# A gated mix of sliding-window attention and a SwiGLU block: x's casts ahead of V's copies, x's sums split on VectorE alone, the gate moved into the last group, more buffers for the projections, a third hidden tile prepared early

## The chip, the cores and the metric

The kernel runs on one core of one Trainium2 chip. The metric is the device time of one execution in microseconds (us).

## What is computed

```python
x = A_x                                             # 1 x 2048 x 512, fp32
g = sigmoid((x * gate_w).sum(-1, keepdims=True))
q, k, v = split_heads(x @ wqkv)                     # 32 heads of 16
s = where(0 <= i - j < 256, q @ k.T / 4, -1e9)      # sliding window of 256
a = (softmax(s) @ v) @ wo
b = (silu(x @ w_gate) * (x @ w_up)) @ w_down        # 512 -> 1792 -> 512
out = g * a + (1 - g) * b
```

## The kernel before

Every fp32 operand of a projection is cut into two halves of precision: `split(hi, lo, src, hi_eng, lo_eng)` (L65) writes a rounded copy hi (a cast) and the rest lo = src - hi (a subtraction), and a product is made of three matmuls: hi hi, hi lo and lo hi. The program is one stream per engine, written out by hand. Each engine runs its own stream in order and waits by semaphores, so an instruction that waits holds up everything behind it on its engine. The same is true of SP, whose queue issues nearly all DMAs, and of POOL, whose queue issues the writes of V and of the attention output. A tile from a pool with n buffers waits until the tile that had its buffer n allocations ago has been read for the last time; when a pool is closed, what is allocated in its place waits for its last readers, DMAs among them. PSUM has four pairs of 128x512 banks: pa, pb, ps1, ps2.

The work comes in five stages.

1. **V** (L169 to L274). x arrives transposed in four chunks c of 512 positions, each in four tiles k. `split_x(c, k)` splits one: the cast on ScalarE (ACT), the subtraction on VectorE (DVE). V's product of block b of 128 positions is twelve matmuls (`vproj`); blocks 0 to 3 need chunk 0, blocks 8 to 11 chunk 2, and so on. `put_v(b)` copies a block from PSUM into one of two buffers `vs` on ACT, and after each second block POOL writes the buffer to DRAM (`vd`). `v_extra(b)` slips other work between: the splits of chunks 2 and 3, the sums of x (`diffs`, on DVE, four tiles for each half a of the positions), their splits (`put_t(a, n, ...)`), and the splits of the first weights (`op_a`, `op_s`, `op_z`).
2. **Q and K** (L364 to L462). Pairs p of head groups, four in all; each pair is a Strassen-Winograd scheme of seven products (numbers 1 to 7) for each half a, six matmuls each. Results are copied out of PSUM by ACT (`copied`, tiles `u`), summed on DVE (`add_to`), split into a `cx` tile (`put_c`: cast on ACT, subtraction on POOL, or on DVE for the product that is taken from PSUM) and written to DRAM (`xd`, 512 KB each) by SP. A product that accumulates into a bank again waits for the copy. The next pair's weights are fetched into the one tile `rw`. The gate's sums (`gate_fetch`, `gate_block`: a 256 KB load of x's rows `xn` and one DVE operation) run here too, four blocks in each pair, and `gate_end` closes them. In the last pair the q and k operands of group 0 begin to be stacked: POOL fills the tiles with constants (`constant_rows`), SP reads `xd` into every fourth row (`stack`, six DMAs for each half and pair of heads).
3. **Start of the attention** (L657 to L676). 64 ticks. In each, three steps of the SwiGLU projections (`stream`, `unit`; results go to DRAM as `raws` through five `ev` buffers), and from tick `WAIT` on, the scores of group 0, whose only use is the row maximum (`stage1`, L557; the maximum on DVE with a mask, L559).
4. **Attention** (L723 to L752). Eight groups of four heads, 16 query blocks t in each, four ticks hd for each block: scores of the next group for their maximum (`stage1`), transposed scores of this one and their exponent (`stage2`, L596, L598), masks on POOL, steps of the projections, and after four blocks the products with V (`av`, L620), taken out of PSUM by `evacuate` and normalized by `finish`. The last group has no scores for a maximum; in it the first eight tiles of `w_down` are split and the first two hidden tiles are made (`tile_early`).
5. **Down projection** (L865 to L898): 56 hidden tiles, each twelve matmuls, and the attention's output projection among them.

A unit of the projections is made by `lanes`: the 128 rows of a matmul are cut into two halves of 64 that run side by side on two result tiles, with one turn over each. The second turn must stand behind a point that the first one's results are known to have passed, and that point is an instruction of the attention's stream:

```python
if second and i == 0:
    tc.add_manual_dep(mm.ins, BEHIND[mark[0]].ins.name, SYNC, reason="the first turn is over")
```

Of the kernel before, what the change touches and what calls it, by code (L numbers as in the profile page):

```python
# [33 lines left out]
def gated_mix(ctx, tc, xT, xn, wqk, wv, wo, wgu, wd, gw, out):  # L34
# [179 lines left out]
    for k in range(NK):  # L214
        split_x(1, k)
    for b in range(4):
        put_v(b, first[b])

# [25 lines left out]
    def v_extra(b):  # L244
        if 4 <= b < 6:
            for k in range(2):
                split_x(2, 2 * (b - 4) + k)
            if b == 4:
                TD.extend(diffs(0))
        elif b < 8:  # L250
            put_t(0, (1, 0)[b - 6], TD[(1, 0)[b - 6]], nc.gpsimd)
        elif b < 10:
            for k in range(2):
                split_x(3, 2 * (b - 8) + k)
        elif b < 12:
            put_t(0, b - 8, TD[b - 8], nc.vector)
        elif b == 12:
# [4 lines left out]
        elif b < 15:  # L262
            put_t(1, (1, 0)[b - 13], TD[(1, 0)[b - 13]], nc.gpsimd)
        else:
            for n in (2, 3):
                put_t(1, n, TD[n], nc.vector)
# [39 lines left out]

    gp = ExitStack()
    gpool = gp.enter_context(tc.tile_pool(name="gpool", bufs=1, side="right"))  # L310
    gwb = gpool.tile([P, D], F32, name="gwb")
    nc.sync.dma_start(gwb, gw[None, :].to_broadcast([P, D]))
    XN = {}

    def gate_fetch(b):
        XN[b] = gpool.tile([P, D], F32, name="xn", bufs=2)
        nc.sync.dma_start(XN[b], xn[b * P:(b + 1) * P])

    def gate_block(b):
        junk = gpool.tile([P, D], F32, name="junk")  # L320
        nc.vector.scalar_tensor_tensor(junk, XN.pop(b), 1.0, gwb, op0=ALU.mult, op1=ALU.mult,
                                       accum_out=gate[:, b:b + 1])

    def gate_end():
        nc.scalar.activation(gate, gate, AF.Exp, scale=-1.0)
        nc.vector.tensor_scalar(gate, gate, 1.0, None, op0=ALU.add)
        nc.vector.reciprocal(gate, gate)
        nc.vector.tensor_scalar(igate, gate, -1.0, 1.0, op0=ALU.mult, op1=ALU.add)
# [21 lines left out]
    def put_c(p, r, c, src, psum):  # L350
        g, (hf, cc) = 2 * p + r, divmod(c, 2)

        def halve():
            cx = cx_tile()
# [70 lines left out]
    for p in range(NP):  # L425
# [34 lines left out]
    gate_end()  # L460
    gp.close()
# [10 lines left out]
    with ExitStack() as A:  # L472
# [3 lines left out]

        constant_rows(1, 0, ("q00", "k00", "q01", "k01"), nc.gpsimd)
        stack(0, 1)
        for hf in range(2):
            constant_rows(hf, 1, ("q10", "k10", "q11", "k11"), nc.gpsimd)  # L480
# [43 lines left out]

        def unit(key):

            def done(hf):
# [5 lines left out]
                return copies  # L533
            (a0, a1), (b0, b1) = (lanes(name, [products(key, 2 * hf + m) for m in range(2)], done(hf))
# [124 lines left out]
        TICKS, WAIT = 16 * NSLOT, 7  # L659
        for n in range(TICKS):  # L660
# [5 lines left out]
            if n == WAIT:  # L666
                stack(1, 0)
            if n == 30:
                stack(1, 1)
# [7 lines left out]

        def wd_early(k, f, piece):
            at(k, lambda: later(4, load_wd(f, pieces[piece], kept())))
# [3 lines left out]
        RAW_AT, TILE_AT = (14, 8), (12, 10)  # L683
        TILE = [None, None]
# [18 lines left out]

        g7 = (G - 1) * NB
        early = chain(tile_early(0), tile_early(1))
# [9 lines left out]
        for n in range(12):  # L715
            at(4 * (g7 + 11) + 1 + 2 * n, lambda: run(early, 1))
# [216 lines left out]
```

## Time and profile before

| | us |
|---|---|
| median of three runs | 859.45 (858.97 to 868.62) |
| the profiled execution | 856.95 |
| its span, first to last instruction | 855.0 |
| PE busy in the span | 824.7 (96%) |
| DVE, ACT, POOL busy | 589.3, 465.2, 385.6 |

The timeline gives start, duration, engine, line and operation, names and shape, and in brackets the idle time before an instruction with what ended it; "x6" is six instructions merged into a row. The chain of waits gives start, duration and what ran or was waited for. Windows give the busy time of each engine in a stretch, the granted clock of TensorE, the busy share of the DMA engines and their GB/s.

### The profile page before, as it was taken

The page shows a single profiled execution, that of the slowest core. Times are in us where ns is not written, and L with a number is a line of the kernel's source. Part 1 is how long each engine was busy: PE and PEld are TensorE (multiplying, and loading weights), DVE is VectorE, ACT ScalarE, POOL GpSimd, SP SyncE. Part 2 cuts the span into 40 slices and gives each one's busy share as a digit, 9 for nine tenths or more (in the row PEclk, how much of TensorE's full clock was granted, in tenths as well). Part 3 has the DMA queues.
Part 4 walks back from the last instruction along what each step waited for, and adds up shares of the span by engine and source line. Part 5 has one row for each costly group of instructions (what it writes and reads, how often), then busy time and mean ns, then how long its engine had stood idle before and what let it go on. Part 6 is the DMA issues. An engine that isn't in the chain of part 4 may idle for free.

```text
span 855.0 us, 21084 instructions
## 1 busy us (share of the span) xinstructions
PE 824.7 (96%) x7945; PEld 681.3 (80%) x7945; DVE 589.3 (69%) x1503; ACT 465.2 (54%) x947; POOL 385.6 (45%) x671
## 2 busy tenths in 40 slices
PE   9796999699999999999999999999998999999998
PEld 7685888588888878787888888888876788888886
DVE  3665664487788888888888888888377764363533
ACT  5452453114676767666666666666766453443441
POOL 5333455603566657656566566565763121101020
PEclk9898999799999999999999999999999999999999
DMA  8335888674255535535455265442547985284741
GB/s 301 99 98 171 308 303 304 230 243 159 71 174 169 166 123 191 179 127 171 161 171 180 90 198 178 143 143 95 178 156 265 299 261 197 81 299 115 232 136 49
DMA packets 78821, 154.21 MB, mean 180 GB/s; under 512 B 12352, under 2 KB 16832, under 8 KB 78720
## 3 DMA queue, kind: packets, MB, share of 16 engines
q1 hardware_dynamic: 74752, 138.97, 49.8%
q0 software_dynamic: 3968, 13.90, 4.5%
q8 instruction: 62, 1.02, 0.5%
q14 instruction: 39, 0.32, 0.1%
HBM read 88.34 MB, written 64.49 MB: 179 GB/s over the span
## 4 chain that ended last, share of the span: by engine, by line
PE 87%; DMA 5%; issue 3%; DVE 3%; SPq 1%; ACT 1%; POOL 1%; DVEq 0%; ACTq 0%; POOLq 0%
PE pa L514 18%; PE pb L514 18%; PE ps L620 9%; PE ps L557 7%; PE ps L81 5%; PE ps L80 5%; PE ps L79 5%; PE ps L596 5%; PE ps L389 3%; PE pb L389 2%; PE pa L389 2%; PE pb L80 2%; PE pb L81 2%; PE pb L79 2%; DMA vd<-vs 1%
## 5 line engine op out<-in xcount | busy, mean ns | idle before, releaser
L559 DVE CUSTOM_DVE_ANT_0 ps<-ps,mask 128x384 f32<-128x384 f32 (+2 forms) x512 | 271.6, 543 | 45.2 <-PE ps L557 34.3
L598 ACT ACTIVATE pt<-ps 128x384 f32<-128x384 f32 (+2 forms) x512 | 238.1, 478 | 80.8 <-PE ps L557 31.9
L596 PE MATMUL ps<-q,k 64*128 64x384 f32 (+2 forms) x512 | 172.0, 347 | 0.8 <-ACT pt L598 0.7
L557 PE MATMUL ps<-k,q 63*128 63x384 f32 (+2 forms) x512 | 163.5, 339 | 0.1
L600 POOL TENSOR_SCALAR_AFFINE_SELECT pt<-pt 128x256 f32<-128x256 f32 x256 | 107.3, 419 | 108.4 <-ACT pt L598 103.3
L557 PEld LDWEIGHTS ps<-k,q 63*128 63x128 f32 x512 | 88.6, 185 | 30.4 <-DVE oe L634 10.8
L514 PE MATMUL pa<-xhi,wh 64*128 64x512 f32 x448 | 101.1, 399 | 8.6 <-DVE mx L559 8.6
L514 PE MATMUL pb<-xhi,wh 64*128 64x512 f32 x448 | 101.5, 394 | 0.0
L596 PEld LDWEIGHTS ps<-q,k 64*128 64x128 f32 x512 | 93.0, 184 | 9.9 <-ACT pt L598 5.8
L514 PE MATMUL pa<-xlo,wh 64*128 64x512 f32 x448 | 100.3, 397 | 0.0
L514 PE MATMUL pb<-xlo,wh 64*128 64x512 f32 x448 | 100.2, 393 | 0.0
L514 PE MATMUL pb<-xhi,wl 64*128 64x512 f32 x448 | 99.3, 391 | 0.0
L514 PE MATMUL pa<-xhi,wl 64*128 64x512 f32 x448 | 98.8, 395 | 0.0
L603 POOL TENSOR_SCALAR_AFFINE_SELECT pt<-pt 128x256 f32<-128x256 f32 x224 | 94.8, 423 | 0.0
L820 DVE TENSOR_TENSOR sg<-got,sg 128x512 f32<-128x512 f32 x53 | 47.1, 889 | 60.9 <-ACT sg L819 59.3
L620 PE MATMUL ps<-pt,vg 64*32 64x320 f32 (+4 forms) x2816 | 76.9, 348 | 0.0
L620 PEld LDWEIGHTS ps<-pt,vg 64*32 64x32 f32 x2816 | 50.7, 106 | 29.3 <-issue 8.4
L637 POOL TENSOR_TENSOR ob<-oe,ob 128x512 f32<-128x512 f32 x32 | 42.1, 1317 | 68.0 <-DVE oe L634 66.7
L559 DVE DVE_READ_ACCUMULATOR2_ANT mx<- 128x1 f32 x512 | 72.3, 141 | 0.0
L514 PEld LDWEIGHTS pa<-xhi,wh 64*128 64x128 f32 x448 | 52.4, 188 | 12.1 <-DVE mx L559 8.8
L67 ACT CAST hh<-sg 128x512 fp32r<-128x512 f32 x54 | 33.3, 617 | 42.9 <-PE ps L80 27.0
L514 PEld LDWEIGHTS pb<-xhi,wl 64*128 64x128 f32 x448 | 53.0, 185 | 3.6
(219 smaller groups left out, 1692.0 us busy)
## 6 DMA issues: line engine op xcount, KB each, us to landing
raws<-ev SPq DMA_DIRECT2D x112, 256.0 KB
got<-raws SPq DMA_DIRECT2D x106, 256.0 KB
xd<-cx SPq DMA_DIRECT2D x32, 512.0 KB
q<-xd SPq DMA_DIRECT2D x96, 128.0 KB
k<-xd SPq DMA_DIRECT2D x96, 128.0 KB
od<-oe POOLq DMA_DIRECT2D x32, 256.0 KB, 3.3
raw<-wgu SPq DMA_DIRECT2D x28, 256.0 KB
vd<-vs POOLq DMA_DIRECT2D x8, 672.0 KB, 4.5
```

The lines of the kernel that those rows point to most:

```text
L79: nc.tensor.matmul(ps, lh, rh, start=start and i == 0, stop=False, skip_group_check=skip)
L80: nc.tensor.matmul(ps, lh, rl, start=False, stop=False, skip_group_check=skip)
L81: nc.tensor.matmul(ps, ll, rh, start=False, stop=stop and i == n - 1, skip_group_check=skip)
L389: nc.tensor.matmul(ps, l[:, w], r[:, k], start=n in (1, 2, 5) and k == m == 0, stop=k == 1 and m == 2, skip_group_check=True)
L514: mm = nc.tensor.matmul(ps[me], w[r], x[r], start=not second and i == 0, stop=bool(second) and i == n - 1)
L557: nc.tensor.matmul(ps[:, :n], QT[g % 2][pr][r, q0:q0 + P], KT[g % 2][pr][r, k0:k0 + n], start=True, stop=True)
L559: mx = nc.vector.tensor_tensor_reduce(out=ps[:, :n], in0=ps[:, :n], in1=mask[:, 3 * P - n:], scale=1.0, scalar=NEG, op0=ALU.add, op1=ALU.m ...
L596: nc.tensor.matmul(ps[:, :n], KT[g % 2][pr][r, k0:k0 + P], QT[g % 2][pr][r, k0:k0 + n], start=True, stop=True)
L598: BEHIND.append(nc.scalar.activation(pt[:, j, :n], ps[:, :n], AF.Exp, scale=SCALE))
L600: nc.gpsimd.affine_select(out=pt[:, :, :P], in_=pt[:, :, :P], pattern=[[0, 2], [1, P]], compare_op=ALU.is_ge, fill=0.0, base=0, channel_mu ...
L603: nc.gpsimd.affine_select(out=pt[:, :, 2 * P:], in_=pt[:, :, 2 * P:], pattern=[[0, 2], [-1, P]], compare_op=ALU.is_ge, fill=0.0, base=-1, ...
L620: nc.tensor.matmul(AV[g, c][h][32 * j:32 * j + 32, q0 - c * CH:q1 - c * CH], VG[4 * g + kb // 4][o, kb % 4, 17 * j:17 * j + 32], PT[g, kb, ...
```

## The change

- In stage 1, `split_x` of chunks 1 and 2 stands ahead of the first four `put_v`, and that of chunk 3 right behind them. `v_extra` keeps the sums and their splits, and all of these have both subtractions and sums on VectorE; one split of a half stands at each of b = 6 to 9 and 12 to 15.
- The gate leaves stage 2. Its loads and sums are made around the last group, every fourth tick (sometimes third), with one buffer for x's rows; the operation comes three ticks behind its load.
- The tiles of `put_c` alternate between the four `cx` and four new `cy` buffers in a pool `more`.
- The first unit of the projections is made by `whole`, without turns: 48 steps of one full matmul. `WAIT` is 10 ticks for 7. Constant rows and stacks of groups 0 and 1 move from ahead of the loop into its ticks 1, 8, 10, 12 and 14.
- In the attention, where `av` stands, four steps of the projections move behind `evacuate`, and the tick behind them has none.
- One hidden tile is made in the last group by `tile_early`; two more by `tile_silu` when the last exponent is through. The down projection starts with three tiles ready for two.

```diff
-    for k in range(NK):
-        split_x(1, k)
+    for c in (1, 2):
+        for k in range(NK):
+            split_x(c, k)
     for b in range(4):
         put_v(b, first[b])
+    for k in range(NK):
+        split_x(3, k)
...
     def v_extra(b):
-        if 4 <= b < 6:
-            for k in range(2):
-                split_x(2, 2 * (b - 4) + k)
-            if b == 4:
-                TD.extend(diffs(0))
-        elif b < 8:
-            put_t(0, (1, 0)[b - 6], TD[(1, 0)[b - 6]], nc.gpsimd)
...
+        if b == 4:
+            TD.extend(diffs(0))
+        elif 6 <= b < 10:
+            n = (1, 0, 2, 3)[b - 6]
+            put_t(0, n, TD[n], nc.vector)
...
+        elif 11 < b:
+            n = (1, 0, 2, 3)[b - 12]
+            put_t(1, n, TD[n], nc.vector)
...
+    more = mp.enter_context(tc.tile_pool(name="more", bufs=1, side="right"))
+    def c_tile():
+        CX[0] += 1
+        return cx_tile() if CX[0] % 2 else more.tile([P, 2, CH], F32R, name="cy", bufs=4)
...
-            if i < 8 and i % 2 == 0:
-                gate_fetch(4 * p + i // 2)
-            if i in (4, 6, 8, 10):
-                gate_block(4 * p + i // 2 - 2)
...
-    gate_end()
-    gp.close()
+    mp.close()
     pro.close()
...
+        def whole(name, todos, done):
+            ps = [pp.tile([P, CH], F32, name=name) for _ in todos]
+            for t, todo in zip(ps, todos):
+                for i, (w, x) in enumerate(todo):
+                    nc.tensor.matmul(t, w, x, start=i == 0, stop=i == len(todo) - 1)
...
-        TICKS, WAIT = 16 * NSLOT, 7
+        TICKS, WAIT = 16 * NSLOT, 10
...
-            if n == WAIT:
-                stack(1, 0)
-            if n == 30:
-                stack(1, 1)
+            if n == 1:
+                constant_rows(1, 0, ("q00", "k00", "q01", "k01"), nc.gpsimd)
+                stack(0, 1)
+            if n in (8, 10, 12, 14):
+                hf, pr = divmod(n // 2 - 4, 2)
+                constant_rows(hf, 1, (f"q1{pr}", f"k1{pr}"), nc.gpsimd)
+                stack(1, hf, (pr,))
...
+        def gate_block(b):
+            t = osb.tile([P, D], F32, name="xn")
+            nc.sync.dma_start(t, xn[b * P:(b + 1) * P])
+            later(3, lambda: nc.vector.scalar_tensor_tensor(t, t, 1.0, gwb, op0=ALU.mult, op1=ALU.mult,
+                                                            accum_out=gate[:, b:b + 1]))
...
+        def tile_silu(n):
+            (gt, up), sg = GOT[n], kept()
+            TILE[n] = halves_of(pieces[TILE_AT[n]])
+            nc.scalar.activation(sg, gt, AF.Silu)
+            nc.vector.tensor_tensor(out=sg, in0=up, in1=sg, op=ALU.mult)
+            split(*TILE[n], sg, nc.scalar, nc.vector)
...
+        at(4 * g7 - 6, lambda: nc.sync.dma_start(gwb, gw[None, :].to_broadcast([P, D])))
+        for b in range(NB):
+            at(4 * g7 - 5 + 4 * b - b // 4, lambda b=b: gate_block(b))
+        at(4 * (g7 + NB - 1), gate_end)
...
-                n = (k + 1) * 9 // 4 - k * 9 // 4
-                if t < G * NB:
+                n = (2, 1, 4, 2)[hd] if values else (k + 1) * 9 // 4 - k * 9 // 4
+                if t < G * NB and not (values and hd == 2):
                     run(steps, n)
                 tick_end()
-                if hd == 1 and part == 0 and t:
+                if hd == 1 and values:
                     av(*divmod(d - 1, NCH))
                     run(FIN, 1)
                     evacuate(*divmod(d - 1, NCH))
+                    if t < G * NB:
+                        run(steps, 4)
...
-        fresh, waiting, ready = [], [(0, n, *TILE[n]) for n in range(2)], []
-        for c, n in seq[2:]:
+        fresh, waiting = [], [(0, n, *TILE[n]) for n in range(3)]
+        ready = [load_wd(8, pieces[8], raw2())]
+        for c, n in seq[3:]:
```

More of the change, by code (lines that the diff above doesn't have):

```diff
@@ L305, in prepare @@
         prefetch()
[L309 to L328, printed above, removed]
+    mp = ExitStack()
+    more = mp.enter_context(tc.tile_pool(name="more", bufs=1, side="right"))
+    CX = [0]
+    def c_tile():
+        CX[0] += 1
+        return cx_tile() if CX[0] % 2 else more.tile([P, 2, CH], F32R, name="cy", bufs=4)
     def fill_rows(t, value, hf, eng):
@@ L533, in done @@
                 return copies
+            if key == UNITS[0]:
+                return chain(*(whole(name, [products(key, 2 * hf + m) for m in range(2)], done(hf))
+                               for hf, name in enumerate(("pa", "pb"))))
             (a0, a1), (b0, b1) = (lanes(name, [products(key, 2 * hf + m) for m in range(2)], done(hf))
@@ L728, in gated_mix @@
             s2 = stage2(g, i) if t < G * NB else iter(())
+            values = part == 0 and t > 0
             for hd in range(4):
@@ L892, in gated_mix @@
                 attn_step(c, n - 8)
-            if len(waiting) > 1:
+            while len(waiting) > (1 if c or n > 5 else 2):
                 step(*waiting.pop(0))
```

47 lines of the change are left out of this document (22 added, 25 removed).

## The prediction

> **What bounds the kernel now.** I read the page first, then windows by stage, then the timeline of PE around each hole, then the other engines and the chain of waits there. Span, clock and GB/s are of the page; then four windows (columns: length, busy PE, PEld, DVE, ACT, POOL, clock, DMA share, GB/s).
>
> ```profile
> span 855.0 us, 21084 instructions
> ...
> PEclk9898999799999999999999999999999999999999
> ...
> GB/s 301 99 98 171 308 303 304 230 243 159 71 174 169 166 123 191 179 127 171 161 171 180 90 198 178 143 143 95 178 156 265 299 261 197 81 299 115 232 136 49
> ...
> 84.00:143.00 59.00, 59.00 (x262) 48.84 (x261) 36.12 (x67) 30.64 (x54) 32.76 (x25) 1.00 0.85 305
> ...
> 203.00:594.00 391.00, 390.81 (x5300) 325.48 (x5298) 329.17 (x1065) 264.13 (x581) 236.09 (x501) 1.00 0.47 152
> 594.00:651.00 57.00, 55.29 (x799) 44.70 (x796) 34.87 (x50) 38.23 (x89) 36.72 (x71) 1.00 0.47 161
> 651.00:678.00 27.00, 24.45 (x102) 18.53 (x103) 22.02 (x36) 13.45 (x23) 5.56 (x5) 1.00 0.93 311
> ```
>
> PE has no idle time in 84 to 143 and next to none in 203 to 594. So TensorE is the bound, its work hardly changes, and what there is to win lies in the holes: three before 164, and small ones behind 594 (57.0 - 55.29 = 1.7 us, 27.0 - 24.45 = 2.55 us). The clock digits dip in the second, fourth and eighth slice, behind the three holes. (A slice is 21.4 us.)
>
> **Term 1, the first hole (x's casts ahead, sums on VectorE).** PE's timeline, with one row of the chain for the pace:
>
> ```profile
> 11.25 1.36 PE pb L208 x6
> ...
> 30.35 0.39 PE L208 MATMUL pa<-wvl,xhi 128*128 128x512 f32 x1
> 33.83 0.79 PE L208 MATMUL pa<-wvh,xlo 128*128 128x512 f32 x1 [3.09 <-DVE xlo L70]
> ...
> 37.08 0.80 PE L208 MATMUL pa<-wvh,xlo 128*128 128x512 f32 x1 [1.60 <-DVE xlo L70]
> ...
> 41.65 0.39 PE L208 MATMUL pb<-wvh,xhi 128*128 128x512 f32 x1
> ```
>
> A 512-column matmul costs 1.36 / 6 = 0.227 us. Between the end of the one at 30.35 (30.58) and 41.65 stand 16 matmuls, block 8 from its third and block 9: 3.63 us of work in 11.07. The hole costs 7.44 us, of which 3.09 + 1.60 are waits for xlo and the rest, 2.7, is half speed behind them. Why xlo was late, on ACT, DVE and POOL:
>
> ```profile
> 23.93 0.59 ACT L183 COPY vs<-ps 128x512 f32<-128x512 f32 x1 [5.26 <-DMA vd<-vs]
> 24.41 1.14 ACT L67 CAST xhi<-k 128x512 fp32r<-128x512 f32 x2
> ...
> 26.28 1.22 DVE L193 TENSOR_TENSOR cx<-q,q 128x1024 f32<-128x1024 f32 x1
> ...
> 30.95 6.08 DVE L70 TENSOR_TENSOR xlo<-k,xhi 128x512 fp32r<-128x512 f32 x2
> ...
> 29.93 3.30 POOL L70 TENSOR_TENSOR q<-cx,q 128x1024 fp32r<-128x1024 f32 x1 [2.70 <-ACT q L67]
> ```
>
> The casts of chunk 2 stood behind block 4's copy, which waited 5.26 us for a write of V; on DVE the four sums came between; and the last two subtractions took 6.08 us for two, where a sum of double the size took 1.22, because they ran against POOL's. After the change the casts follow those of chunk 1, bound only by x's arrival: chunk 2 ends the first 16 transfers of 0.26 MB, 14 us at the 301 GB/s of the first slice, so with the start some 15.5; casts and subtractions end near 17, eleven us ahead of block 8, whose first matmul stands eight ahead of 30.35, at 28.5. The copies of blocks 0 to 3 slip 1 to 2 us; their banks are wanted by block 8 only. DVE takes four subtractions of some 1.22 us from POOL; its list up to the last block is then 16 of half that size, 16 of 1.22 and about 4 us for the weights, 34 us in 45. Block 15's half is due for product 7, seven us after V's end. So I cost all of this at nothing; the cover is those seven us of products; with it gone, it would be one subtraction, 1.2 us. **-7.4**, bounds -7.4 and -4.
>
> **Term 2, the second hole (the gate leaves SP).** PE, POOL, a step of the chain, SP and ACT:
>
> ```profile
> 63.18 0.39 PE L389 MATMUL ps<-xhi,al 128*128 128x512 f32 x1
> ...
> 77.72 1.22 PE L389 MATMUL pb<-k,sh 128*128 128x512 f32 x2 [6.66 <-ACT u L373]
> ...
> 83.56 0.62 PE L389 MATMUL pa<-k,zh 128*128 128x512 f32 x2
> ...
> 59.65 6.71 POOL L70 TENSOR_TENSOR q<-cx,q 128x1024 fp32r<-128x1024 f32 x2 [3.25 <-ACT q L67]
> ...
> 66.31 4.17 DMA vd<-vs
> ...
> 70.62 0.33 SPq L312 DMA_DIRECT2D gwb<-gw  x1
> 71.11 0.80 SPq L127 DMA_DIRECT2D rw<-wqk  x2
> ...
> 76.04 0.62 ACT L67 CAST ah<-rw 128x512 fp32r<-128x512 f32 x1 [6.80 <-DMA rw<-wqk]
> ```
>
> From 63.41 to 83.56 stand eight products of six matmuls, 10.88 us in 20.15: the hole costs 9.27. PE waited for a copy on ACT that stood behind a cast of the next weights, these had been fetched at 71.11 only, behind the gate's own load on SP, and that load took the place of V's buffers, whose last write left POOL at 66.31, after two subtractions of 6.71 us. The change takes away every link: no load for the gate here, no subtraction of these on POOL. What is late next is the first `cy` tile, which takes V's place now: from 41.65 on V has 72 matmuls, 16.3 us, so it ends at 58.0 - 7.4 = 50.5; its last write is issued by 52 and needs 4 to 5 us (4.17 above), and the `cy` cast belongs to the fourth product, four times 1.36 later, and stands behind a copy of the fifth: near 58. **-9.3**, bounds -9.3 and -6.
>
> **Term 3, the third hole (start of the attention).** PE, a step of the chain, DVE and ACT:
>
> ```profile
> 143.50 0.59 PE L514 MATMUL pa<-xhi,wh 64*128 64x512 f32 x2
> ...
> 149.09 0.29 PE L557 MATMUL ps<-k,q 63*128 63x128 f32 x2
> 157.94 0.79 PE L514 MATMUL pa<-xhi,wh 64*128 64x512 f32 x2 [8.56 <-DVE mx L559]
> ...
> 163.59 1.38 PE pb L514 x12
> ...
> 153.01 3.00 DVE L326 TENSOR_SCALAR gate<-gate 128x16 f32<-128x16 f32 x1 [7.68 <-ACT gate L325]
> ...
> 157.53 0.30 DVE L559 CUSTOM_DVE_ANT_0 ps<-ps,mask 128x128 f32<-128x128 f32 x1 [0.61 <-DMA xd<-cx]
> ...
> 152.24 0.62 ACT L67 CAST cx<-u 128x512 fp32r<-128x512 f32 x1 [3.93 <-DMA xd<-cx]
> ```
>
> A step takes 1.38 / 6 = 0.23. From the end of the scores at 149.2 to 163.59 stand twelve steps and two pairs of scores, 2.96 us in 14.39: 11.4 lost. A second turn waited for the first maximum; that one stood behind the gate's end on DVE, behind casts that waited for `cx` buffers, and last for the final `xd` write, since its own tile lies where stage 2's tiles lay. The change takes away the turns of unit 0 (33 steps, 7.6 us, come ahead of the first scores), the casts' waits (eight buffers) and the gate's end. **-11.4**, and two things are late next (SP's timeline, and the page's issues):
>
> ```profile
> 166.65 1.72 SPq L341 DMA_DIRECT2D q<-xd  x3
> ...
> xd<-cx SPq DMA_DIRECT2D x32, 512.0 KB
> ```
>
> First, the last writes. In new time stage 2 ends at 143.5 - 16.7 = 126.8. The last sum, cast and subtraction take 0.7 + 0.6 + 1.3, so the last five writes of 0.52 MB leave SP near 128 to 131, behind six stacks, and at 305 GB/s (84 to 143) need 8.6 us: landed at 137 to 139. The first maximum waits for that; PE needs it for the fifth score matmul, tick 15, behind 45 steps at 137.5, and the copies to `ev` need the same place by the 48th, 138.5. I take **+1.5**, bounds 0 and +4 (with half speed). Second, SP: 36 transfers of the stacks at 1.72 / 3 = 0.57 us each stand ahead of or between unit 0's four results now, 21 us from 130.5 on; the last result leaves near 152 and takes some 3.3 us (`od`, below), and unit 2, 108 steps and 25 ticks of scores in, needs that `ev` buffer's bank by 154.5. **+0.5**, bounds 0 and +3.
>
> The clock behind such waits: 3.09 us (of 30.35) was followed by half speed, 1.03 us (650.82, below) by none. At 1.5 us, nearer to the second, I take none; 2.7 more, as behind the first hole, is in the upper end. [...]
>
> **Term 4, attention.** Group by group PE does the same work. Moving four steps behind `evacuate` covers the wait of the following scores for the evacuation, but puts two score pairs next to each other, which then want two maxima in a row. Rows for this and the next two terms, from the page's groups, the waits (total, times, longest), the issues (the last number is from issue to landing), a window's groups (84 to 143) and the timeline:
>
> ```profile
> L559 DVE CUSTOM_DVE_ANT_0 ps<-ps,mask 128x384 f32<-128x384 f32 (+2 forms) x512 | 271.6, 543 | 45.2 <-PE ps L557 34.3
> ...
> PEld ps L557 <- DVE oe L634: 10.8, 27, 0.5
> ...
> od<-oe POOLq DMA_DIRECT2D x32, 256.0 KB, 3.3
> ...
> L321 DVE SCALAR_TENSOR_TENSOR junk<-xn,gwb 128x512 f32<-128x512 f32 x13 | 10.6, 813 | 19.5 <-DMA xn<-xn 19.5
> ...
> 634.14 3.35 DVE L697 RECIPROCAL ev<-ev 128x512 f32<-128x512 f32 x1
> ...
> 650.82 0.50 PE L79 MATMUL ps<-q,k 128*128 128x512 f32 x1 [1.03 <-ACT ob L633]
> ```
>
> The wait named is 10.8 / 27 = 0.4 us; a maximum takes 0.54. The old wait goes, one of about 0.2 to 0.4 comes two ticks later: **0**, bounds -7 and +10.
>
> **Term 5, the last group.** Sixteen loads on SP, each waiting for the operation before it (one buffer), 16 x 0.8 = 13 us on DVE. A 256 KB transfer takes 3.3 us by POOL's rows; with 0.8 for the operation a block needs 4.1 us, and its spacing is 3.75 ticks of at most 56 / 64 = 0.87 (594 to 650), 3.3 us. So at worst SP falls 13 us behind, and the projections' results behind it, their `ev` buffers, then PE's banks. For less speaks that half of the DMA is free there (0.47) and that SP's queue has little else to do. One early tile less also takes a reciprocal of 3.35 us out of DVE, which is busy 35 of 57 us there. I take **+1**, bounds -2 and +12.
>
> **Term 6, the third tile.** The wait of 1.03 at the turn to stage 5 and the 2.55 of its ramp are 3.6 us. One tile more is 2.7 us more cover for loads at 311 GB/s, the bound of the ramp; but both silu tiles now stand on ACT and DVE ahead of the last evacuation, which waits about 1 us longer. **-2**, bounds -3.6 and +2.
>
> **The sum.** -7.4 - 9.3 - 11.4 + 1.5 + 0.5 + 0 + 1 - 2 = **-27.1 us**. Of the profiled execution's 856.95 that leaves 829.9; the median of the runs is 2.5 higher, 859.45, so I predict **832** for the median. For this one core 2% is 17 us, 842.3: what a measurement tells from no change.
>
> **The rivals.**
>
> - *The start still waits (841).* The last write lands late, or SP's 36 stacks hold the `ev` buffers: of the third hole 6 us stay, and 3 of half speed. For it: the DMA's 0.85 busy share ahead of that place. Against it: 4.2 MB of the gate's loads leave this stretch. Chance 0.13.
> - *The gate holds the last group (844).* Term 5 at its end, 12 us. For it: in 84 to 143 thirteen such operations waited 19.5 us for their loads, with two buffers. Against it: there the DMA was at 0.85. Chance 0.12.
> - *A hole of V or Q and K stays (839).* The change doesn't do what it says: x arrives later than I think, or the `cy` tile waits for V's last write, 7 us. For it: block 4's copy still waits for a write of V. Against it: nothing that PE needs stands behind that copy any more. Chance 0.05.
> - *The attention is better (824).* The evacuation's wait of 10.8 us goes and no new one comes. Chance 0.1.
> - *Slower (882).* One place: the two adjacent score pairs behind each of 28 `av`. PE stands in order; if the tick behind them waits until DVE has taken out the evacuation, a transpose (128x512, at most 0.81 as the gate's operation) and two maxima, 2 x 0.81 + 2 x 0.54, less four steps of cover, 0.92, that is 1.8 us for each, 50 us in all: 832 + 50. It decides from 27 / 28 = 1 us for each on. Against it: DVE is not the bound in 203 to 594 (329 of 391 busy), and the pair wants one maximum, not two. Chance 0.03.
>
> **How the numbers follow.** My forecast, 826 to 838, has 0.57. The range, 822 to 845, takes in four rivals and leaves out the slow one and the tails. Faster by over 2% (under 842.3): 0.56 of the forecast, 0.09 of the first rival, 0.04 of the second, 0.05 and 0.1, together 0.84. Slower by over 2% is the far end of the last rival, 0.02; the rest, 0.14, is within 2%.
>
> **What would show it.** V's matmuls without a gap up to 50.5; the first product of Q and K there, the first step of the projections at 127 (143.5 before); exponents from 176 on, where the first maxima are through. The clock at full speed from 6 us on: a dip near 138 or 156 speaks for the first rival. In the last group, 53 us from the first `av` of group 6's end to the last one; SP waiting for x's rows, or ACT's copies for `ev`, speaks for the second. It would be wrong if PE idled between 203 and 594 of the old order, or if the three holes came back at other places.

## The result: slower by one per cent, and the profile after

The changed kernel takes 869.8 us (median of 16 runs, 866.5 to 873.1) beside 861.9 of the kernel before on the same chip (16 runs, 855.2 to 870.1): a ratio of 1.0105, 95% interval 1.0075 to 1.0135. The ratio and its interval leave out four executions of before that lie more than 1.5% above its fastest. The forecast was 832. The profiled execution took 870.03 us.

The clock digits of after's page first, then rows of its chain of waits and of PE's timeline at the places that the prediction named:

```profile
PEclk9999999899999999999999999999888999999999
```
```profile
50.85 1.36 PE pa L368 x6
...
200.91 1.88 PE ps L602 x56
...
542.35 1.88 PE ps L602 x56
```
```profile
126.85 0.39 PE L499 MATMUL pa<-xhi,wh 128*128 128x512 f32 x1
...
662.54 0.74 PE L79 MATMUL ps<-q,k 128*128 128x512 f32 x1 [2.26 <-ACT ob L615]
```

Two rows of before's chain that the prediction did not need stand beside them (first products with V of group 0 and of group 6):

```profile
217.33 1.88 PE ps L620 x56
...
552.87 1.88 PE ps L620 x56
```

Read together they give a ledger, in us from the start of each span:

| place | before | after | difference |
|---|---|---|---|
| first step of the projections | 143.50 | 126.85 | -16.6 |
| first product with V, group 0 | 217.33 | 200.91 | -16.4 |
| first product with V, group 6 | 552.87 | 542.35 | -10.5 |
| first product of stage 5 | 650.82 | 662.54 | +11.7 |
| end of the span | 855.0 | 868.0 | +13.0 |

So the first two holes closed as forecast, the third gained nothing, each of six groups became 1.0 us longer (55.9 to 56.9, the stretch between the second and third row divided by six), and the last stretch, from group 6's first products with V to stage 5, lost 22 us. Of the clock digits the two dips of the second and fourth slice are gone, the one of the eighth (152 to 174) is 8 where before had 7, and three new ones stand at 608 to 673, in the last group and the turn to stage 5.

**The start of the attention.** PE, ACT and SP of after:

```profile
155.03 0.49 PE L483 MATMUL pa<-xhi,wh 64*128 64x512 f32 x1 [1.56 <-ACT ev L510]
160.74 0.70 PE L483 MATMUL pb<-xhi,wh 64*128 64x512 f32 x1 [2.16 <-ACT ev L510]
164.62 0.79 PE L483 MATMUL pb<-xhi,wh 64*128 64x512 f32 x1 [3.18 <-ACT ev L510]
```
```profile
160.11 0.58 ACT L510 COPY ev<-pb 128x512 f32<-128x512 f32 x1 [5.13 <-DMA raws<-ev]
```
```profile
134.04 3.31 SPq L320 DMA_DIRECT2D q<-xd  x3
...
151.50 0.52 SPq L511 DMA_DIRECT2D raws<-ev  x1
...
155.86 0.53 SPq L511 DMA_DIRECT2D raws<-ev  x1
...
159.23 1.81 SPq L322 DMA_DIRECT2D k<-xd  x3
161.14 0.60 SPq L511 DMA_DIRECT2D raws<-ev  x1
```

SP issues stack transfers from 134.04 to 161.04, and single results of the projections come out between them. ACT's copy needs one of five `ev` buffers, these are freed by the results' writes, and PE needs the bank that ACT empties.

**The last group.** The lost stretch as a window of before and of after:

```profile
552.87:650.82 97.95, 96.23 (x1358) 78.25 (x1357) 70.38 (x162) 65.37 (x150) 61.48 (x124) 1.00 0.44 150
```
```profile
542.35:662.54 120.19, 103.76 (x1359) 83.07 (x1359) 78.36 (x195) 67.71 (x154) 63.67 (x124) 0.94 0.49 156
```

For the same matmuls PE was idle for 16.4 us where it had been for 1.7, and busy for 7.5 us more at a mean granted clock of 0.94. So some 15 us are waits, and most of the rest is half speed behind them (granted clock 0.50 from 609 to 614, 639 to 642 and 649 to 652). Waits from 584 to 700 (total, times, longest), then DVE and SP at one place, ACT at that place and at a second one, and four waits of PE:

```profile
DVE xn L668 <- DMA xn<-xn: 21.5, 10, 3.0
ACT ob L615 <- DVE ot L626: 20.3, 4, 7.5
```
```profile
602.85 0.69 DVE L668 SCALAR_TENSOR_TENSOR xn<-xn,gwb 128x512 f32<-128x512 f32 x1 [2.89 <-DMA xn<-xn]
...
606.36 0.69 DVE L668 SCALAR_TENSOR_TENSOR xn<-xn,gwb 128x512 f32<-128x512 f32 x1 [1.74 <-DMA xn<-xn]
...
606.97 0.71 DVE L626 STREAM_TRANSPOSE ot<-ob 128x512 f32<-128x512 f32 x1
```
```profile
603.58 0.33 SPq L667 DMA_DIRECT2D xn<-xn  x1
```
```profile
607.77 0.53 ACT L615 COPY ob<-ps 128x448 f32<-128x448 f32 x1 [7.38 <-DVE ot L626]
...
635.43 0.63 ACT L694 ACTIVATE ev<-k 128x512 f32<-128x512 f32 x1 [3.34 <-DMA k<-raws]
```
```profile
608.75 1.06 PE L578 MATMUL ps<-q,k 64*128 64x384 f32 x2 [5.83 <-ACT pt L580]
...
626.57 0.82 PE L578 MATMUL ps<-q,k 64*128 64x384 f32 x2 [1.92 <-ACT pt L580]
...
636.98 0.82 PE L578 MATMUL ps<-q,k 64*128 64x384 f32 x2 [3.16 <-ACT pt L580]
...
648.45 0.97 PE L578 MATMUL ps<-q,k 64*128 64x384 f32 x2 [2.81 <-ACT pt L580]
```

One operation of the gate ends at 603.54, SP issues the next load at 603.58, and the next operation starts at 606.36: 3.5 us a block, most of it the load. The transpose stands behind that operation, ACT's copy to the one `ob` waits for the transpose (7.38 us), the exponents stand behind the copy, and PE waits 5.83 us for an exponent. That chain crosses four engines, each of which works in order. The waits of 1.92 and 2.81 us stand behind later copies to `ob`, which waited 5.00 and 7.45 us for a transpose. The wait of 3.16 us has another way: ACT's exponent of the early tile waited 3.34 us for its load, which SP issued at 630.97, right behind a load of the gate at 630.07 that had waited for VectorE.

### The profile page after: what moved, and what is told of

Same layout as the page of the kernel before. It is cut to its first block, busy times and chain, and to the rows that moved or that the text cites. A ratio compares the mean times of both kernels' runs of the same rounds, so it can differ in the third digit from the quotient of the medians.

```text
span 868.0 us, 20987 instructions
## 1 busy us (share of the span) xinstructions
PE 834.5 (96%) x7897; PEld 687.4 (79%) x7897; DVE 579.1 (67%) x1504; ACT 465.5 (54%) x947; POOL 376.0 (43%) x667
## 4 chain that ended last, share of the span: by engine, by line
PE 80%; DMA 5%; DVE 5%; POOL 3%; SPq 2%; issue 2%; ACT 1%; DVEq 0%; POOLq 0%; ACTq 0%
PE pb L483 15%; PE pa L483 15%; PE ps L602 8%; PE ps L539 6%; PE ps L81 5%; PE ps L79 5%; PE ps L80 5%; PE ps L578 4%; DMA xn<-xn 3%; PE ps L368 3%; PE ps L208 3%; PE pa L368 2%; PE pb L368 2%; PE pb L79 2%; PE pb L80 2%
## 5 line engine op out<-in xcount | busy, mean ns | idle before, releaser
L580 ACT ACTIVATE pt<-ps 128x384 f32<-128x384 f32 (+2 forms) x512 | 234.4, 478 | 99.9 <-PE ps L578 55.1
L578 PE MATMUL ps<-q,k 64*128 64x384 f32 (+2 forms) x512 | 166.7, 346 | 13.9 <-ACT pt L580 13.7
L539 PEld LDWEIGHTS ps<-k,q 63*128 63x128 f32 x512 | 92.4, 184 | 31.7 <-DVE mx L541 22.8
L483 PE MATMUL pb<-xhi,wh 64*128 64x512 f32 x432 | 106.8, 409 | 5.3 <-ACT ev L510 5.3
L483 PE MATMUL pa<-xhi,wh 64*128 64x512 f32 x432 | 104.8, 407 | 1.6 <-ACT ev L510 1.6
L483 PE MATMUL pb<-xlo,wh 64*128 64x512 f32 x432 | 105.2, 400 | 0.0
L483 PE MATMUL pb<-xhi,wl 64*128 64x512 f32 x432 | 103.8, 397 | 0.0
L483 PE MATMUL pa<-xlo,wh 64*128 64x512 f32 x432 | 102.6, 398 | 0.0
L483 PEld LDWEIGHTS pb<-xhi,wh 64*128 64x128 f32 x432 | 56.6, 188 | 11.6 <-ACT ev L510 6.2
L483 PEld LDWEIGHTS pb<-xhi,wl 64*128 64x128 f32 x432 | 57.5, 188 | 3.1
```

Source lines behind the costliest of these rows:

```text
L483: mm = nc.tensor.matmul(ps[me], w[r], x[r], start=not second and i == 0, stop=bool(second) and i == n - 1)
L539: nc.tensor.matmul(ps[:, :n], QT[g % 2][pr][r, q0:q0 + P], KT[g % 2][pr][r, k0:k0 + n], start=True, stop=True)
L578: nc.tensor.matmul(ps[:, :n], KT[g % 2][pr][r, k0:k0 + P], QT[g % 2][pr][r, k0:k0 + n], start=True, stop=True)
L580: BEHIND.append(nc.scalar.activation(pt[:, j, :n], ps[:, :n], AF.Exp, scale=SCALE))
```

## The experiments

Thirteen kernels, all built from after. Medians in us; the ratio is to the kernel before, with its 95% interval. Before's own runs spread from 854.5 to 869.6, so steps between variants are read from the variants' medians (their runs, 4 to 10 of each, lie within 0.5% of these) and from their traces. The variants were timed in four groups on four chips, each beside before, whose fastest run took 854.5 to 856.6 us in each group; a step of one or two us between kernels of different groups is not told from none. In kernels with the second row buffer, line numbers from 55 on are one higher than in after.

| kernel | median | ratio to before |
|---|---|---|
| after | 869.8 | 1.011 (1.008 to 1.014) |
| two_rows | 855.1 | 0.992 (0.989 to 0.996) |
| one_load | 851.7 | 0.989 (0.986 to 0.993) |
| late_stacks | 861.2 | 1.001 (0.997 to 1.004) |
| old_steps | 863.5 | 1.001 (0.997 to 1.005) |
| three_fixes | 841.1 | 0.976 (0.970 to 0.982) |
| early_turn | 886.1 | 1.031 (1.026 to 1.036) |
| four_fixes | 859.2 | 0.997 (0.993 to 1.000) |
| early_turn_last | 836.8 | 0.977 (0.974 to 0.980) |
| old_x_order | 845.9 | 0.984 (0.979 to 0.989) |
| pool_sums | 851.9 | 0.993 (0.990 to 0.996) |
| four_cx | 842.4 | 0.983 (0.981 to 0.986) |
| unit0_lanes | 848.3 | 0.990 (0.987 to 0.992) |
| two_tiles | 841.0 | 0.977 (0.970 to 0.984) |

### The last group: two_rows and one_load

```
-    mask = const.tile([P, 3 * P], F32, name="mask")
+    xn1 = const.tile([P, D], F32, name="mask")
+    mask = xn1[:, :3 * P]
 ...
-            t = osb.tile([P, D], F32, name="xn")
+            t = xn1 if b % 2 else osb.tile([P, D], F32, name="xn")
```

> The kernel after, with a second buffer for the rows of x that the gate reads in the last group: the mask's own tile, widened to 512 columns, which only the first six and a half groups read. Theory A (one buffer makes a chain: load, operation, load, so that the operations come late and the transposes, the copy to ob, the exponents and PE stand behind them): first product of stage 5 at 643 to 646 instead of 662.5, time 851 to 853 (-17 to -19). Theory B (the sixteen operations' own time on VectorE, about 0.7 us each, is what delays the transposes, however the rows come in): 866 to 870 (0 to -4). Theory C (SP's queue stands still at the gate's transfers and the other transfers behind it are late): as A in time, but then the waits for xn vanish and those for ev and raw too.

```
-            t = osb.tile([P, D], F32, name="xn")
-            nc.sync.dma_start(t, xn[b * P:(b + 1) * P])
+            if b == 0:
+                XN.append(osb.tile([P, D], F32, name="xn"))
+                nc.sync.dma_start(XN[0], xn[b * P:(b + 1) * P])
+            t = XN[0]
```

> The kernel after, with the first of the sixteen loads of x's rows only: the sixteen operations all read that block, so 15 loads are left out and the gate's sums are those of block 0. Tells the loads from the operations. Theory A (the chain of load and operation through one buffer): 849 to 854, as with two buffers or a little better. Theory B (the operations' own 0.7 us each on VectorE): 866 to 870.

Measured: 855.1 (-14.7) and 851.7 (-18.1). PE's first product of stage 5, of two_rows and then of one_load:

```profile
650.24 0.50 PE L80 MATMUL ps<-q,k 128*128 128x512 f32 x1 [2.24 <-ACT ob L616]
```
```profile
647.77 0.50 PE L79 MATMUL ps<-q,k 128*128 128x512 f32 x1 [2.25 <-ACT ob L615]
```

Theory A holds and B falls: all sixteen operations are still there in one_load, and 18 us are gone with the loads. The second buffer brings most of that, less than the expected 17 to 19, and stage 5 starts at 650 rather than 643 to 646: the transposes still stand behind other work on VectorE, which early_turn_last takes up below. C holds for one wait of the five: the wait for the early tile's load (3.34 us on ACT in after) is in neither of these two traces. By way of `ev`, C held nothing in after, where ACT has no wait for `ev` between 545 and 665.

### The start: late_stacks

```
-            if n in (8, 10, 12, 14):
-                hf, pr = divmod(n // 2 - 4, 2)
-                constant_rows(hf, 1, (f"q1{pr}", f"k1{pr}"), nc.gpsimd)
-                stack(1, hf, (pr,))
+            if n in (WAIT, 30):
+                hf = n // 30
+                constant_rows(hf, 1, ("q10", "k10", "q11", "k11"), nc.gpsimd)
+                stack(1, hf)
```

> The kernel after, with group 1's constant rows and its 24 transfers put back to two steps (ticks 10 and 30, twelve each) from ticks 8, 10, 12, 14. Theory A (SP's 36 transfers in one run of 27 us, ahead of unit 0's results, keep the five ev buffers full, ACT's copies wait, PE waits 1.6, 2.2 and 3.2 us and its clock falls): first product with V at 191 to 194 instead of 200.9, time 861 to 863 (-7 to -9). Rival B (what holds the start is that unit 0 runs in whole products and the scores come between; the transfers have nothing to do with it): 868 to 871 (0).

Before the change group 1's transfers stood inside the loop as well, at ticks 7 and 30; only group 0's last twelve transfers and the constant rows stood ahead of it.

Measured: 861.2 (-8.6). The only wait of PE for `ev` that is left, and group 0's first product with V:

```profile
155.17 0.50 PE L483 MATMUL pa<-xhi,wh 64*128 64x512 f32 x1 [1.52 <-ACT ev L510]
```
```profile
193.30 1.88 PE ps L602 x56
```

Theory A to the number: 193.30 beside 200.91, the second and third wait gone.

### The groups' pace: old_steps

```
-                n = (2, 1, 4, 2)[hd] if values else (k + 1) * 9 // 4 - k * 9 // 4
-                if t < G * NB and not (values and hd == 2):
+                n = (k + 1) * 9 // 4 - k * 9 // 4
+                if t < G * NB:
 ...
-                    if t < G * NB:
-                        run(steps, 4)
```

> The kernel after, with the old spacing of the projection steps in attention: 9 steps to each 4 ticks, always spread the same, none kept back behind the products with V. Theory A (the new spacing lets pairs of scores meet, which makes PE wait for the maximum): a group takes 55.9 us again, not 56.9, time 863 to 865 (-5 to -7). Rival B (the group is longer because other work of the change reaches into it, so that the spacing costs nothing): 869 to 871 (0). Rival C (the spacing gains behind the products with V, where exponents would stand first): 872 to 876.

Measured: 863.5 (-6.3). Windows over six groups, of after and then of old_steps (length, busy PE and so on):

```profile
200.91:542.35 341.44, 339.50 (x4616) 278.92 (x4623) 280.46 (x909) 225.89 (x499) 205.72 (x431) 1.00 0.48 155
```
```profile
202.67:537.88 335.21, 335.16 (x4616) 278.14 (x4623) 282.06 (x911) 226.95 (x499) 203.91 (x431) 1.00 0.49 158
```

The same 4616 matmuls take 341.44 / 6 = 56.9 and 335.21 / 6 = 55.9 us a group. Of the 6.2 us only 1.9 are idle time of PE (341.44 - 339.50); the rest is longer busy time, at a granted clock of 1.00 in both. What the scores waited for shows in the loads of their weights into TensorE (PEld), over the same two windows (total, times, longest):

```profile
PEld ps L539 <- DVE mx L541: 18.3, 41, 0.5
```
```profile
PEld ps L539 <- DVE oe L616: 9.4, 24, 0.5
...
PEld ps L539 <- DVE mx L541: 4.2, 17, 0.2
```

In after 41 waits for a maximum take 18.3 us; in old_steps 41 waits take 13.6, and 24 of these are for the evacuation (`oe`). Theory A holds: the waits for the evacuation went, and longer ones for the maximum came.

### All three: three_fixes

> The three edits together: second buffer for the gate's rows, group 1's transfers at two later steps, old spacing of the steps. If the three losses are separate, their gains add: -17 to -19, -7 to -9, -5 to -7, so 836 to 841, which would be some 22 us faster than the kernel before and near what the prediction gave. If one loss only uncovers another (the start's gain is taken again by the group's pace, or the last group has its own bound on DVE): 845 to 855.

Measured: 841.1, at the slow end of the first range. The three gains sum to 29.6 and together give 28.7: the losses were separate. This version is 2.4% faster than before (1.8% to 3.0%).

### What is left of the link: early_turn, four_fixes, early_turn_last

```
                 if hd == 1 and values:
                     av(*divmod(d - 1, NCH))
-                    run(FIN, 1)
+                    if t <= g7:                  # early_turn_last only
+                        run(FIN, 1)
                     evacuate(*divmod(d - 1, NCH))
 ...
+                if hd == 1 and part == 2:        # early_turn_last: and t > g7
+                    run(FIN, 1)
```

> The kernel after, with one edit: the first half of finish (transpose ob to ot, reciprocal, product) is put two slots (8 ticks, some 7 us) earlier in the order, ahead of the next products with V rather than behind them. One buffer for x's rows stays. Theory A (the gate's late operations cost time only by the link transposes -> the one ob buffer -> ACT's copy -> exponents -> PE): the waits of ACT for ot (20.3 us in 584 to 700) and of PE for pt (5.83, 1.92, 3.16, 2.81) mostly go; first product of stage 5 at 646 to 650 instead of 662.5, time 855 to 859 (-11 to -15). Rival B (the late operations hold PE by another way, such as ev buffers that the DVE's splits of wd keep, or the loads on SP): 866 to 870.

> The three edits of three_fixes and the earlier transposes together. In three_fixes PE still waits 3.51 us at 590.97, 1.50 at 621.00 and 2.24 at 635.09, each behind a copy to ob that waits for transposes which stand behind other work on VectorE, with the clock at 0.88 to 0.89 around them. Theory: all three go, with the half speed behind them: 832 to 835 (-6 to -9 against three_fixes' 841.1). Rival (in the last group VectorE has too much to do anyway, 11 to 12 of each 14 us, and the waits only move): 839 to 842.

Measured: 886.1 and 859.2, 16.3 and 18.1 us slower where 11 to 15 and 6 to 9 faster were expected. DVE and PE of four_fixes in a middle group:

```profile
275.14 0.57 DVE L542 CUSTOM_DVE_ANT_0 ps<-ps,mask 128x384 f32<-128x384 f32 x1 [0.24 <-PE ps L579]
...
275.78 0.57 DVE L542 CUSTOM_DVE_ANT_0 ps<-ps,mask 128x384 f32<-128x384 f32 x1
...
276.26 0.71 DVE L627 STREAM_TRANSPOSE ot<-ob 128x512 f32<-128x512 f32 x1
...
277.64 0.56 DVE L542 CUSTOM_DVE_ANT_0 ps<-ps,mask 128x384 f32<-128x384 f32 x1
```
```profile
278.31 0.44 PE L540 MATMUL ps<-k,q 63*128 63x384 f32 x1 [0.53 <-DVE mx L542]
```

In the first seven groups the maxima come in runs of one every 0.64 us (275.14, 275.78). The three operations (276.26 to 277.64, 1.38 us) now stand inside such a run and PE waits for the maximum behind them; behind the products with V they stood between two runs. This I had not priced: I had looked at the last group alone, which has no maxima.

In that last group the rival of early_turn has its part. ACT no longer waits for `ot` there, yet PE still waits 4.69 and 3.58 us for an exponent. ACT and PE of early_turn at the first:

```profile
636.08 0.59 ACT L510 COPY ev<-pb 128x512 f32<-128x512 f32 x1 [4.68 <-DMA raws<-ev]
```
```profile
637.12 1.07 PE L578 MATMUL ps<-q,k 64*128 64x384 f32 x2 [4.69 <-ACT pt L580]
```

ACT's copy to `ev` stands ahead of the exponents and waits for a buffer. The two results that should have freed buffers were copied by 625.58 and left SP at 632.77, behind two loads of the gate (629.04 and 632.35) that each waited for VectorE. At the second place ACT waits 3.75 us for the early tile's load, which SP issues too. So the gate's loads hold PE by SP's queue as well; in after that shows in one wait only, the 3.16 us.

> three_fixes (841.1) with the earlier transposes in the last group alone, where no maxima stand on VectorE. From the last products with V of group 6 to the last but one of group 7 four_fixes took 593.70 to 649.58, 55.9 us, three_fixes 570.80 to 630.36, 59.6. Theory (the transposes -> ob -> ACT -> exponents link is what is left of the gate's price, and only the maxima made the earlier place dear): -3.7 there, and most of the 2.24 us at the turn to stage 5, so 834 to 837. Rival (the wait at the turn is set by the third tile's own work on VectorE): 837 to 839.

Measured: 836.8 (-4.3), the upper end of the theory's range. Of the waits of 3.51, 1.50 and 2.24 us in three_fixes these are left, beside one of 0.63:

```profile
592.83 0.83 PE L579 MATMUL ps<-q,k 64*128 64x384 f32 x2 [1.37 <-ACT pt L581]
...
630.04 0.50 PE L80 MATMUL ps<-q,k 128*128 128x512 f32 x1 [1.83 <-ACT ob L616]
```

So, with two buffers, most of what was left of the gate's price in the last group was the link; the wait at the turn mostly stays (1.83), as the rival had it.

### Parts of the gain put back, on three_fixes: old_x_order, pool_sums, four_cx, unit0_lanes

```
old_x_order:  split_x(2, .) with blocks 4 and 5, split_x(3, .) with blocks 8 and 9
pool_sums:    the same, and put_t(., n, TD[n], (nc.gpsimd, nc.vector)[n > 1])
four_cx:      return cx_tile()                                       # in c_tile
unit0_lanes:  if False:  # for key == UNITS[0];   TICKS, WAIT = 16 * NSLOT, 7
```

> three_fixes (841.1) with the old order of x's casts and subtractions: chunk 1 ahead of V's copies, chunk 2 with blocks 4 and 5, chunk 3 with blocks 8 and 9; VectorE keeps all subtractions of the sums. Theory A (PE's first hole came from the casts' place behind V's copies, which wait for V's writes): the hole of 7.4 us is back, first products of Q and K at 57 to 58, time 847 to 849. Rival B (it came from the subtractions that ran against POOL's, 6.08 us for two; with POOL's gone the order alone does little): products of Q and K at 51 to 53, time 841 to 843.

> three_fixes with the old order of x's splits, as in old_x_order (845.9), and also POOL doing half of the subtractions of the sums again, as before the change. Theory A (it was the pair that made the first hole: late casts on ACT and subtractions that run against POOL's at 3 us each): PE waits of 3 and 1.6 us for xlo are back with half speed behind them, first product of Q and K at 57 to 58, time 850 to 854. Rival B (POOL's share is harmless): as old_x_order, 51.5 and 845 to 847.

Measured: 845.9 and 851.9. DVE of old_x_order, then DVE, POOL and PE of pool_sums at the same work:

```profile
30.40 1.28 DVE L71 TENSOR_TENSOR xlo<-k,xhi 128x512 fp32r<-128x512 f32 x2
```
```profile
29.87 6.10 DVE L71 TENSOR_TENSOR xlo<-k,xhi 128x512 fp32r<-128x512 f32 x2
```
```profile
28.86 3.33 POOL L71 TENSOR_TENSOR q<-cx,q 128x1024 fp32r<-128x1024 f32 x1 [2.70 <-ACT q L68]
...
33.05 2.36 POOL L71 TENSOR_TENSOR k<-cx,k 128x1024 fp32r<-128x1024 f32 x1
```
```profile
32.78 0.72 PE L209 MATMUL pa<-wvh,xlo 128*128 128x512 f32 x1 [1.92 <-DVE xlo L71]
```

Two subtractions took 1.28 us with POOL quiet and 6.10 against POOL's two of 3.33 and 2.36, and only then was the first hole back: the products of Q and K start at 51.39 in old_x_order and at 57.32 in pool_sums, beside 50.98 in three_fixes. So with the old order POOL's share made the hole, and with POOL quiet the old order costs 0.4 us there. The new order with POOL's share was not run. In after VectorE is through with chunk 3's subtractions at 21.9 us, seven ahead of POOL's first one in pool_sums (28.86), so that the order alone would probably have closed the hole too. How POOL's work slowed VectorE's was not shown.

pool_sums tells something of the second hole as well. POOL's subtractions are back in it, and from the first product of Q and K to the first step of the projections it takes 76.0 us (57.32 to 133.32), as three_fixes does (50.98 to 126.98). So POOL's share alone doesn't bring that hole back. It stands a block earlier here, though: V's last write leaves POOL 2.8 us behind the first product of Q and K (60.07), where it had left 8.3 behind it in before (66.31 against 57.97). And no run puts the gate's load back, so which link made the second hole stays open.

The time of old_x_order (+4.8) fits neither theory. Most of it stands at one wait for `ev`, which took 1.36 us in three_fixes:

```profile
156.49 0.79 PE L484 MATMUL pa<-xhi,wh 64*128 64x512 f32 x1 [3.39 <-ACT ev L511]
```

Half speed follows it (granted clock 0.52 from 156.5 to 163). Why it is longer stays open: four_fixes and two_tiles, whose start is the same code as that of three_fixes, have it at 2.35 and 2.67 us.

> three_fixes with four buffers for the split projections, as before the change, where there are eight. Theory A (with four, the last casts wait for xd writes, so that the last writes and the first maximum come late): casts wait 3 to 4 us each near the end of stage 2, first maximum at 141 to 143 instead of 138.4, PE waits there and its clock falls, time 844 to 849. Rival B (the writes' own time at some 300 GB/s sets the first maximum, not the buffers): 840 to 842.

> three_fixes with unit 0 in lanes (two turns of half the rows, the second one bound to the maximum ahead of it) and the first scores at tick 7, as before the change; the transfers of the stacks stay where three_fixes has them. Theory A (PE has nothing to do until the first maximum, at 138.4 by the last xd writes, once the first turns, some 24 steps from 127 on, and two scores are through): PE waits 3 to 5 us for a maximum near 133 to 138, half speed for some 3 us behind it, time 845 to 849. Rival B (the start is bound by the ev buffers now, so that the wait only moves ahead of them): 840 to 842.

Measured: 842.4 and 848.3. Four buffers, ACT and PE:

```profile
129.28 0.62 ACT L68 CAST cx<-u 128x512 fp32r<-128x512 f32 x1 [3.96 <-DMA xd<-cx]
```
```profile
140.86 0.83 PE L540 MATMUL ps<-k,q 63*128 63x256 f32 x2 [2.34 <-DVE mx L542]
```

The casts' wait is back as theory A had it, and PE waits 2.34 us for a maximum (0.79 in three_fixes). The profiled execution is 3.05 us behind three_fixes at the first product with V (196.61 beside 193.56), yet the median is only 1.3 higher: from group 6's first products with V to stage 5 this execution is 2.3 us shorter, where the two kernels are the same code. So the eight buffers are worth some 3 us at the start by this one trace, and the medians don't tell it from nothing. Lanes for unit 0 bring the third hole back:

```profile
138.64 0.80 PE L484 MATMUL pa<-xhi,wh 64*128 64x512 f32 x2 [6.36 <-DVE mx L542]
```

Theory A holds for the lanes together with the earlier first scores (+7.2), with a longer wait than the 3 to 5 us expected. The profiled execution is the fastest of the four: it is 5.0 us slower than that of three_fixes, and 4.1 of these lie between the first step and the first product with V.

### The third tile: two_tiles

The turn to stage 5 as before the change (two early tiles by exponents, `run(FIN)` ahead of what is left over), on early_turn_last.

> early_turn_last (836.8) with the turn to stage 5 as before the change: two tiles halved ahead, both by exponents in the last group (two reciprocals of 3.35 us), the last transposes ahead of what is left over, waiting list of one. Theory A (three tiles cover the ramp of stage 5, as Term 6 had it): it gets slower by 2 to 4, 839 to 841. Rival B (the third tile's work stands on ACT and VectorE ahead of the last copy to ob, and takes back what it covers): 834 to 837.

Measured: 841.0 (+4.2), theory A's upper end. The profiled executions differ by 6.3 us: 4.3 behind the first product with V (840.9 - 195.75 against 834.5 - 193.67), and 2.1 ahead of it, where the two kernels are the same code. So the 4.3 is the better figure, and it rests on one trace of each.

## Why the prediction was wrong, step by step

- **Term 1 (-7.4): right.** Q and K start at 50.85 where 57.97 stood: -7.1, and PE has no wait of over 0.4 us in V. I had given the casts' order and POOL's two subtractions as one chain. The runs show that taking POOL's share out is enough to break it; the order alone was not run.
- **Term 2 (-9.3): right in time.** -16.6 at the first step, less Term 1, is -9.5. Which link of its chain made the hole is not shown: POOL's subtractions alone did not bring it back (pool_sums), and the gate's load was not put back.
- **Term 3 (-11.4 + 1.5 + 0.5): the last part failed.** The turns of unit 0 made the wait of the third hole (unit0_lanes), and the first maximum came at 138.37 as forecast. The failed step is "the last result leaves near 152": it put 36 transfers at 0.57 us from 130.5 on. They began at 134.04, with 3.31 us for the first three, took some 27 us and were through at 161.04; unit 0's four results left at 151.50, 155.86, 161.14 and behind. The term was **+0.5** with an end of +3; by late_stacks it is **8.6** (7.6 in the traces), of which half speed (granted clock 0.50 from 161 to 167) behind waits of 1.56, 2.16 and 3.18 us in a row is a part. The rival "The start still waits" had just this mechanism and 9 us, at a chance of 0.13.
- **Term 4 (0): wrong in size, inside its bounds.** 1.0 us a group, 6.3 in all. I set the new wait equal to the old one that it replaced; the weight loads of the scores waited 18.3 us in six groups of after and 13.6 with the old spacing.
- **Term 5 (+1, to +12): the main error, 18 by one_load.** The size of the chain was there (4.1 us a block against 3.3; 3.5 in the trace), and 13 us of lag was its worst case; the term took 1 of them, and I followed the lag along SP only, to `ev`. The step that failed is what stands behind the waiting instruction: on VectorE it is the transposes, and behind these one `ob` buffer, ACT's exponents and PE. So the price is not a lag to be caught up by the end of the group, but a wait behind three of the products with V, and the first product of stage 5 waits as well. SP's queue, the way that I did follow, took a smaller part: one wait of 3.16 us in after, and more once the transposes are out of the way (early_turn).
- **Term 6 (-2): not found.** From the first product of stage 5 to the end before took 204.2 us with two tiles; with three it is 203.4 (three_fixes) to 205.5 (after), so no gain stands clear of that spread. two_tiles took 208.1 there, so the old turn would now cost 4; of the 3.9 that it takes more than before, a wait of 2.08 us for the evacuation (`oe`) at 635.87 is a part, and the rest is open.
- **The rivals.** Terms 3 and 5 as rivals, and Term 4, came true at once. I had laid the rivals' chances side by side, as if one of them could come at a time; they sit in different stages, and three_fixes shows that they add (29.6 singly, 28.7 together). 841 - 832 = 9 for the first and 12 for the second would with Term 4's end of +10 have given 863; nothing in my range (822 to 845) stood for the sum.

With the three losses mended the sum of what the change wanted comes to 841.1, and to 836.8 with the transposes earlier in the last group.

## What to carry to other kernels

When work is moved to a stage that looks half empty, follow each waiting instruction on its own engine: list what stands behind it in order, which single buffers these free, and who waits for those, until the chain reaches the bound engine. A one-buffer load is a loop of load and operation, 3.5 us a block here; VectorE's busy share, 78.36 of 120.19 us in after's last stretch, did not show it, and a second buffer, here in a tile that the stage no longer reads, took away 14.7 us of the 18.1 that went with the loads. Risks in different stages add, so a range must hold their sum.

## What the runs showed of the hardware that I had not expected

A wait's length alone did not tell whether the clock fell. The same wait at the same place, 2.24 us in two_rows and 2.25 us in one_load, was followed by these rows (two_rows, then one_load):

```profile
651.36 0.63 PE L80 MATMUL ps<-q,k 128*128 128x512 f32 x1
```
```profile
648.58 0.39 PE L79 MATMUL ps<-q,k 128*128 128x512 f32 x1
```

The fourth matmul behind the wait took 0.63 us in the first and 0.39 in the second, and the next one started 0.42 and 0.22 us behind it: half speed and full speed. I had gone by two rows of before, a granted clock of 0.50 behind 3.09 us and of 1.00 behind 1.03. Here 1.52 us alone (late_stacks) brought none, the matmuls behind it taking 0.39 us; 3.39 (old_x_order) did, with a granted clock of 0.52; and between them it went either way: behind the 2.35 us of four_fixes at the start of the attention the granted clock stayed at 1.00, behind the 2.67 us of two_tiles at the same place it was 0.57. No one length parts these waits: 2.24 us had half speed behind it, 2.25 and 2.35 had not. What else decides was not shown.
